# Mixing from two copies of V: the low-rank part kept once, the second copy swapped by transfers within SBUF

## The chip, the cores and the metric

The kernel runs on one core of one Trainium2 chip. The metric is the device time of an execution in microseconds; the time before is 667.36 us, the median of three runs. A core has a matrix engine (PE, with its weight loads listed apart as PEld), a vector engine (DVE), a scalar engine (ACT), GpSimd (POOL) and SyncE (SP), which here only issues transfers. Each engine runs its own list of instructions in order; semaphores tie the lists together.

## The reference, cut to what matters

```python
# attention: 4 batches, 8 heads, 768 positions, head size 64, decay lam per head
intra = np.einsum('bhic,bhjc->bhij', qb, kb) * Dmask[None]
intra = np.einsum('bhij,bhjd->bhid', intra, vb)
inter = np.einsum('bhid,bhde->bhie', qb * lam_pow[None], kv_state)
out[:, :, sl] = intra + inter
...
# mixer: x is the attention's output as (4, 768, 512); U is 768 x 32, V is 32 x 768
xt = x.transpose(0, 2, 1)
h = xt @ U @ V
u = x + h.transpose(0, 2, 1)
ch = np.maximum(u @ w_ch1, 0.0) @ w_ch2
return (u + ch).astype(np.float32)
```

The change touches `h`: along the 768 positions of a batch, P = xᵀU has rank 32, and the mix is Vᵀ times P, one 128 x 512 tile of u at a time.

## The kernel before, in words

The 4 x 768 rows are 24 tiles of 128, numbered s = 6b + c (batch b, tile c). The attention takes one tile per step. The list `pieces` (L637 to L667) writes the order of a step out by hand: transposes of q and k for tile s+1 (`prep`, L368), the turn and the mix of earlier tiles, the attention's products for tile s (`intra`, `state`, `inter`), scores for tile s+1 (`scores`), then side work (`aside`, L734: conversion of weights from double precision, one piece at a time). Each engine gets its instructions in exactly this order.

At the end of a batch `low` (L469) multiplies its six tiles by U into a 32 x 512 result. `low_rows` (L487) splits that result into a high part (the upper bits) and a low part (the rest), and the pieces in `pps`, called as `next_of_low` (L542) in the first step of the next batch, put them where the mix reads them. The mix of tile s runs in step s + 7, so the first is in step 7 and reads what step 6 wrote.

All products of the mix are of high and low parts, four in number: high V and low V, each with high P and low P. Half the columns of the result come from rows 0 to 63 of the operands, the other half from rows 64 to 127. `v_hl` (L290) holds V on 4 x 32 rows: high, low, high, low. `p_hl` holds, for each half of 64 rows, the high part of P twice (columns 0 to 255) and the low part twice (columns 256 to 511). `mix` (L552) makes four matmuls per tile: for the high columns and then the low columns, one for each half of the rows; as the 64 rows of V are high over low, each matmul sums two of the products.

Filling `p_hl` for one batch (L525 to L538) takes four ACT copies of the high part (`spread`, L527), two POOL subtractions for the low part (L531) and two ACT copies that double the low part (`spread_low`, L538). `spread` and `low_part` are called ahead of `scale` in the step, `spread_low` after `mixed`. The last batch is mixed during the first product with w_ch1, with a full 128-row `p_hl` (L492 to L511, L566).

V itself is prepared by `v_steps` (L682) as side work of steps 0 to 5: a load in two parts of 32 rows, the conversion on DVE and ACT, then the high part by four ACT copies (L706) and the low part by two DVE (L710, rows 32 to 63) and two POOL subtractions (L710, rows 96 to 127), both in step 5.

Loads on SP are issued by `load_next` (L670) in the same order: q and k in `prep`, v in `next_v` (L435), each into buffers (three for q and v, four for k) that an earlier tile has left. The words of the weights (L140) and the stores of finished tiles u (L577) stand on the same SP list.

`v_hl` and `p_hl` are columns of one tile, `vp` (L289), in a slot of the pool of w_ch1's weights; two further columns of it hold constants for the conversion (`set_ends`, L751). `lam_row` (L747) and `blank` (L748) are used before the first step only.

After the attention (some 117 us) come the products with w_ch1 (L817, L827) and with w_ch2 (L950 to L954).

Of the kernel before, what the change touches and what calls it, by code (L numbers as in the profile page):

```python
# [8 lines left out]
FP32 = mybir.dt.float32  # L9
F32R = mybir.dt.float32r  # L10
# [4 lines left out]
P = 128  # L15
# [3 lines left out]
def kernel(  # L19
# [28 lines left out]
    nc = tc.nc  # L48

    B, H, S, D = q.shape  # L50
    HP = H // 2
    NT = S // P
    C = H * D
# [3 lines left out]
    R = moe_U.shape[1]  # L57
    G = P // R
# [29 lines left out]
    def set_ends(t):  # L88
        nc.vector.memset(t[:, 0:1], 1151.0)
        nc.vector.memset(t[:, 1:2], 255.0 * (1 << 23))  # L90
        ends.append(t)
# [195 lines left out]

    assert G == 4
    vp = w1_pool.tile([P, 3, C], F32R, tag="w1", name="vp").rearrange("p n c -> p (n c)")  # L289
    v_hl, p_hl = vp[:, 0:S], vp[:, S : S + C]  # L290


    ident = keep.tile([P, P], FP32, name="ident")
    small = consts.tile([P, 16], FP32, name="small")
    zeros = small[:, 0:1]

    mask = consts.tile([P, 2, HP, P], FP32, name="mask")
# [189 lines left out]
    def low_rows(b):  # L487

        pp, t = pps.pop(b), tmp("p_h")[0:R]
        own = [(slice(g * R, (g + 1) * R), slice(g * P, (g + 1) * P)) for g in range(G)]  # L490
        if b == B - 1:
            h, h2, l, l2 = (p_hl[g * R : (g + 1) * R] for g in range(G))  # L492
            for rows, cols in own:
                nc.vector.tensor_scalar(
                    t[:, cols].bitcast(U32), pp[rows].bitcast(U32), HI, None, ALU.bitwise_and
                )

            def low_part():
                for rows, cols in own:
                    nc.vector.tensor_tensor(  # L500
                        out=l[:, cols], in0=pp[rows], in1=t[:, cols], op=ALU.subtract
                    )

            def spread():
                nc.scalar.copy(h, t)
                nc.scalar.copy(h2, t)

            def spread_low():
                nc.scalar.copy(l2, l.bitcast(FP32))

            pps[b] = [spread, low_part, spread_low]  # L511
            return

        rows_f, pp = pp, others.pop(b)
        for g in range(2, G):
            nc.vector.tensor_copy(
                out=rows_f[:, g * P : (g + 1) * P], in_=pp[g * R : (g + 1) * R]
            )
        nc.vector.tensor_scalar(t.bitcast(U32), rows_f.bitcast(U32), HI, None, ALU.bitwise_and)
        wide = [slice(x * 2 * P, (x + 1) * 2 * P) for x in range(2)]  # L520

        def place(g, low):
            return p_hl[g * R : (g + 1) * R, wide[low]]

        def spread():  # L525
            for g in range(G):
                nc.scalar.copy(place(g, 0), t[:, wide[g // 2]])  # L527

        def low_part():
            for x in range(2):  # L530
                nc.gpsimd.tensor_tensor(  # L531
                    out=place(2 * x, 1), in0=rows_f[:, wide[x]], in1=t[:, wide[x]],
                    op=ALU.subtract,
                )

        def spread_low():
            for x in range(2):
                nc.scalar.copy(place(2 * x + 1, 1), place(2 * x, 1).bitcast(FP32))  # L538

        pps[b] = [spread, low_part, spread_low]  # L540

    def next_of_low(b):  # L542
        pps[b].pop(0)()
# [7 lines left out]

    def mix(s):  # L552
        b, c = divmod(s, NT)
        weights = v_hl[:, c * P : (c + 1) * P]
        if b < B - 1:
            pm = both_halves(s)[:, :, 2 * P :]
            for low in range(2):
                for x in range(2):
                    nc.tensor.matmul(  # L559
                        out=pm[:, x], lhsT=weights[half[x]],  # L560
                        rhs=p_hl[half[x], low * 2 * P : (low + 1) * 2 * P],
                        start=(low == 0), stop=(low == 1),
                    )
            return
        pu = bank([P, C], "pu", "b2")
        nc.tensor.matmul(out=pu, lhsT=weights, rhs=p_hl, start=True, stop=True)  # L566
        nc.vector.tensor_tensor(out=xs[s], in0=pu, in1=xs[s], op=ALU.add)

    def mixed(s):
# [68 lines left out]
    for s in range(NS):  # L638
        b, c = divmod(s, NT)
        done = s - NT - 1  # L640
        more = s + 1 < NS
        turns = done > 0 and (done - 1) // TG < FG
        mixes = 0 <= done < NS - NT - 1
        rows = c == 0 and b > 0
        step = [("prep", s + 1)] * more
        step += [("turn", done - 1)] * turns + [("mix", done)] * mixes
        step += [("mix", done + 1)] * (not more)
        step += [("next_of_low", b - 1)] * rows + [("next_of_low", b - 1)] * rows
        step += [("scale", s + 1)] * more
        step += [("fade", s)] * (c > 0)  # L650
        step += [("late", s - 1)] * (1 < s < NT - 1 or s > NT)
        step += [("turned", done - 2)] * (done > 1 and c == 1)
        step += [("split", done - 1)] * turns
        step += [("mixed", done)] * mixes + [("mixed", done + 1)] * (not more)
        step += [("next_of_low", b - 1)] * rows
        both = [("intra", s), ("state", s)]
        step += (both if s > NT else both[::-1]) + [("next_v", s), ("inter", s)]
        step += [("late", s)] * (s < 2 or s in (NT - 1, NT))
        step += [("turned", done - 1)] * (done > 0 and c > 0)
        step += [("scores", s + 1)] * more  # L660
        step += [("low", b)] * (more and c == NT - 1)
        step += [("aside", s)] * (0 < s < NT - 2 or s > NT)
        step += [("masked", s + 1)] * more
        step += [("low_rows", b)] * (more and c == NT - 1)
        step += [("aside", s)] * (s in (0, NT - 2, NT - 1, NT))
        step += [("store", done)] * (done >= 0 and done // TG < FG)
        pieces += step  # L667
# [14 lines left out]
    def v_steps():  # L682
# [8 lines left out]
        def parts(gs):  # L691
            for half in range(2):
                rows, cols = slice(half * R, (half + 1) * R), slice(half * SH, (half + 1) * SH)
                for g in gs:
                    yield v_hl[g * R : (g + 1) * R, cols], rows

        def five():
            st["t"] = t = wconv.tile([P, C], FP32, tag="wt", name="vt")[0 : 2 * R, 0:SH]
# [9 lines left out]
        def low(g, engine):  # L708
            for out, rows in parts((g,)):
                engine.tensor_tensor(  # L710
                    out=out, in0=st["v"][rows], in1=st["t"][rows], op=ALU.subtract
                )

        halves = [moe_V[:, half * SH : (half + 1) * SH] for half in range(2)]
        return weight_steps(dst, halves, SH, 2 * R, in_parts=True) + [
            five, lambda: low(1, nc.vector), lambda: low(3, nc.gpsimd),
# [27 lines left out]

    ordered = ctx.enter_context(ExitStack())
    ordered.enter_context(tc.manual_schedule())
    lam_row = consts.tile([1, H + P], FP32, name="lam_row")  # L747
    blank = x_pool.tile([P, C], FP32, tag="x", name="blank")[:, 0:P]  # L748
    nc.vector.memset(blank, 0.0)
    nc.vector.memset(lam_row[:, H:], 1.0)  # L750
    set_ends(vp[:, S + C : S + C + 2].bitcast(FP32))  # L751
    nc.scalar.dma_start(out=lam_row[:, 0:H], in_=lam.unsqueeze(0))
    load_next("q", nc.sync)
    load_next("k", nc.scalar)
# [299 lines left out]
```

## Time and profile before

| what | us |
|---|---|
| median of three runs | 667.36 (666.33 to 668.0) |
| the profiled execution | 669.62 |
| its span, first to last instruction | 667.8 |
| L559, mix of three batches: 72 matmuls, 72 weight loads | 316 ns and 188 ns each (median) |
| L527, ACT copies of the high part: 12 | 404 ns each |
| L531, POOL low part: 6 | 724 ns each |
| L538, ACT copies of the low part: 6 | 402 ns each |
| L710, DVE low part of V: 2 | 766 ns each |
| L710, POOL low part of V: 2 | 1000 ns each |

The profile is of one execution. Times are from the span's start; L numbers are lines of the kernel before. A stretch "40.00:60.00" lists busy time and number of instructions of PE, PEld, DVE, ACT and POOL, then the granted clock of PE, the busy share of the DMA engines and GB/s. In the timeline a line gives start, duration, engine, line, operation, output and inputs; a bracket gives idle time of the engine ahead of it and what released it. The DMA rows of the timeline show issuing on SP, not the transfer.

### The profile page before, as it was taken

To read this page: it belongs to the slowest core of one execution; us is meant where nothing else is said; L and a number is where in the kernel's file an instruction comes from. 1 tells how busy PE (TensorE), PEld (TensorE's weight loads), DVE (VectorE), ACT (ScalarE), POOL (GpSimd) and SP (SyncE) were. 2 spreads that over 40 slices of the span, in tenths; PEclk is the share of its full clock that TensorE was granted. 3 is DMA by queue.
4 is the path that set the end of the run, shared out by engine and by line. 5 is a ranking of instruction groups with operands and counts; after the bars stand their busy time and mean duration, and the time that the engine had idled before them with its cause. 6 is when DMAs were issued, how large, how long until landed. Compare 5 with 4: busy or idle time off the path is not lost.

```text
span 667.8 us, 13404 instructions
## 1 busy us (share of the span) xinstructions
PE 656.2 (98%) x5242; PEld 538.7 (81%) x5242; DVE 491.0 (74%) x862; ACT 280.4 (42%) x530; POOL 115.0 (17%) x98
## 2 busy tenths in 40 slices
PE   8899999999999999999999999999999999999997
PEld 7788988788888888888888887888888888888886
DVE  5578988878999777777797255786677776865864
ACT  4677885554555444444453121332322322322320
POOL 4465876330000000000000000030030300300300
PEclk9999999999999999999999999999999999999999
DMA  8999984355776655555578899764263453543531
GB/s 197 224 224 233 259 217 139 127 190 162 268 249 238 216 199 202 201 201 200 201 263 292 311 326 395 253 212 126 89 211 104 125 190 94 168 147 96 159 93 63
DMA packets 131776, 131.29 MB, mean 197 GB/s; under 512 B 81346, under 2 KB 89794, under 8 KB 131714
## 3 DMA queue, kind: packets, MB, share of 16 engines
q1 hardware_dynamic: 130512, 130.05, 62.2%
q8 instruction: 41, 0.67, 0.4%
q10 hardware_dynamic: 1202, 0.39, 0.2%
q14 instruction: 21, 0.17, 0.1%
HBM read 80.09 MB, written 50.33 MB: 195 GB/s over the span
## 4 chain that ended last, share of the span: by engine, by line
PE 95%; DMA 1%; DVE 1%; SPq 1%; issue 1%; ACT 0%; DVEq 0%; ACTq 0%
PE pz L817 27%; PE pz L950 13%; PE pz L952 13%; PE pd L827 13%; PE pd L954 13%; PE px L447 3%; PE pss L406 3%; PE px L458 2%; PE pqk L358 2%; DMA qraw<-in_q_dram 1%; PE pkv L425 1%; SPq L279 1%; PE pp L474 1%; PE pm L559 1%; PE put L590 1%
## 5 line engine op out<-in xcount | busy, mean ns | idle before, releaser
L817 PE MATMUL pz<-u_hl,w 128*128 128x512 f32 x768 | 190.0, 397 | 0.0
L817 PEld LDWEIGHTS pz<-u_hl,w 128*128 128x128 f32 x768 | 144.0, 188 | 35.2 <-ACT r L823 0.3
L952 PE MATMUL pz<-w_hl,m 128*128 128x512 f32 x384 | 151.1, 396 | 0.0
L950 PE MATMUL pz<-w_hl,m 128*128 128x512 f32 x384 | 150.9, 396 | 0.0
L954 PE MATMUL pd<-w_d,m 128*128 128x512 f32 x384 | 149.5, 396 | 0.0
L933 ACT ACTIVATE m<-mt 128x512 fp32r<-128x512 f32 x96 | 60.6, 632 | 196.6 <-PE pd L954 127.5
L979 POOL TENSOR_TENSOR o<-o,u 128x512 f32<-128x512 f32 x20 | 29.9, 1531 | 447.4 <-DMA rm<-r_d 291.4
L934 DVE SCALAR_TENSOR_TENSOR m<-rm,m 128x512 fp32r<-128x512 f32 x96 | 71.4, 745 | 47.3 <-ACT m L933 47.2
L832 DVE SCALAR_TENSOR_TENSOR r<-pd,r 128x512 f32<-128x512 f32 x96 | 61.8, 685 | 53.5 <-ACT r L823 43.5
L827 PE MATMUL pd<-u_d,w 128*128 128x512 f32 x384 | 98.6, 397 | 0.0
L823 ACT ACTIVATE r<-pz 128x512 f32<-128x512 f32 x96 | 52.1, 596 | 93.0 <-PE pz L817 92.3
L952 PEld LDWEIGHTS pz<-w_hl,m 128*128 128x128 f32 x384 | 72.3, 188 | 17.8 <-DVE m L934 0.2
L954 PEld LDWEIGHTS pd<-w_d,m 128*128 128x128 f32 x384 | 72.3, 188 | 17.7 <-DVE m L935 0.2
L950 PEld LDWEIGHTS pz<-w_hl,m 128*128 128x128 f32 x384 | 72.3, 188 | 17.6
L827 PEld LDWEIGHTS pd<-u_d,w 128*128 128x128 f32 x384 | 72.1, 188 | 17.3
L932 DVE TENSOR_SCALAR mt<-rm 128x512 uint32<-128x512 uint32 x96 | 46.1, 481 | 33.5 <-DMA rm<-r_d 33.2
L935 DVE SCALAR_TENSOR_TENSOR m<-m 128x512 fp32r<-128x512 f32 x96 | 69.1, 721 | 0.9
L415 DVE TENSOR_TENSOR sm<-pss,mask 128x512 f32<-128x512 f32 x48 | 30.9, 684 | 10.0 <-PE pss L406 9.7
L212 ACT CAST w<-wt 128x512 fp32r<-128x512 f32 x32 | 19.8, 620 | 30.6 <-DVE wt L209 23.4
L406 PE MATMUL pss<-qt,kt 64*128 64x128 f32 x384 | 29.1, 291 | 0.8 <-issue 0.7
L447 PE MATMUL px<-vraw,sm 128*64 128x64 f32 x768 | 27.8, 225 | 1.2 <-ACT x_nat L464 0.6
L447 PEld LDWEIGHTS px<-vraw,sm 128*64 128x64 f32 x768 | 24.9, 138 | 3.9 <-ACT x_nat L464 0.9
(96 smaller groups left out, 668.7 us busy)
## 6 DMA issues: line engine op xcount, KB each, us to landing
r_d<-r SPq DMA_DIRECT2D x96, 256.0 KB, 2.4
rm<-r_d SPq DMA_DIRECT2D x96, 256.0 KB, 2.7
words<-in_moe_w_ch_dram SPq DMA_DIRECT2D x30, 512.0 KB, 4.3
w_d<-w SPq DMA_DIRECT2D x16, 768.0 KB, 3.3
w_hl<-w_d SPq DMA_DIRECT2D x16, 512.0 KB, 6.4
vraw<-in_v_dram SPq DMA_DIRECT2D x24, 256.0 KB, 5.0
u_d<-x_nat SPq DMA_DIRECT2D x24, 256.0 KB, 4.1
u<-u_d SPq DMA_DIRECT2D x24, 256.0 KB, 4.1
```

The source lines that it names most:

```text
L406: nc.tensor.matmul(out=pss[:, x, a, :], lhsT=kt[half[x], a, :], rhs=qt[half[x], a, :], start=True, stop=True,)
L447: nc.tensor.matmul(out=px[half[t], x, a, :], lhsT=sm[:, x, a, half[t]], rhs=vr[:, 2 * a + x, :], start=(a == 0), stop=(alone and a == HP - 1),
L817: nc.tensor.matmul(out=acc[g][0], lhsT=w[:, n, ct, :], rhs=uhl[g][:, n, ct, :], start=(ct == 0 and n == 0), stop=(ct == CT - 1 and n == 1),)
L823: nc.scalar.mul(rs[g], acc[g][0], 4096.0 + 1.0)
L827: nc.tensor.matmul(out=acc[g][1], lhsT=w[:, 2, ct, :], rhs=ud[g][:, ct, :], start=(ct == 0), stop=(ct == CT - 1),)
L832: nc.vector.scalar_tensor_tensor(rs[g], acc[g][1], 4096.0, rs[g], ALU.mult, ALU.add)
L933: nc.scalar.activation(out=m[:, 0], in_=t, func=AF.Relu)
L934: nc.vector.scalar_tensor_tensor(m[:, 1], r, 0.0, hi, ALU.max, ALU.subtract)
L935: nc.vector.scalar_tensor_tensor(m[:, 2], hi, E, low, ALU.mult, ALU.subtract)
L950: nc.tensor.matmul(out=pz, lhsT=m[:, 0, cols], rhs=hl[:, 0], start=first, stop=False)
L952: nc.tensor.matmul(out=pz, lhsT=m[:, 1, cols], rhs=hl[:, 1], start=False, stop=end)
L954: nc.tensor.matmul(out=pd, lhsT=m[:, 2, cols], rhs=dd, start=first, stop=end)
```

## The change

A second copy of V, with high and low exchanged in each pair of 32 rows, is kept beside the first: `v_hl` is now two copies of 768 columns, which fill `vp`. `p_hl` becomes a tile of its own of 256 columns with, for each half of 64 rows, the high part over the low part, each once. The mix again makes four matmuls per tile of the same shapes: for the plain V and then the swapped V, one for each half of the rows. Plain V gives high by high and low by low, swapped V gives the two cross products.

For one batch this needs two ACT copies in place of four, the same two POOL subtractions, and no `spread_low`. The swapped copy is made once, by four transfers of 32 x 768 elements from SBUF to SBUF, issued on SP at the head of step 6. In the lists of the engines these four transfers stand after the words of step 5's side work and ahead of the q load of step 6. The first reads what DVE's L710 wrote, the third what POOL's wrote, the second and fourth what ACT's L706 wrote. On PE the third matmul of the first mix waits for the first and second transfer, the fourth for the third and fourth.

The last batch's P goes into the second copy of V, which no mix reads by then. The constants of `set_ends` move to `small`, and `lam_row` into the tile of `blank`.

```diff
-    v_hl, p_hl = vp[:, 0:S], vp[:, S : S + C]
+    v_hl = vp.rearrange("p (n c) -> p n c", n=2)
+    p_hl = consts.tile([P, 2 * P], F32R, name="p_hl")
...
-    small = consts.tile([P, 16], FP32, name="small")
+    small = consts.tile([P, 18], FP32, name="small")
...
-            h, h2, l, l2 = (p_hl[g * R : (g + 1) * R] for g in range(G))
+            h, h2, l, l2 = (v_hl[g * R : (g + 1) * R, 1, 0:C] for g in range(G))
...
-        def place(g, low):
-            return p_hl[g * R : (g + 1) * R, wide[low]]
+        def place(g):
+            return p_hl[g * R : (g + 1) * R]
 
         def spread():
-            for g in range(G):
-                nc.scalar.copy(place(g, 0), t[:, wide[g // 2]])
+            for x in range(2):
+                nc.scalar.copy(place(2 * x), t[:, wide[x]])
 
         def low_part():
             for x in range(2):
                 nc.gpsimd.tensor_tensor(
-                    out=place(2 * x, 1), in0=rows_f[:, wide[x]], in1=t[:, wide[x]],
+                    out=place(2 * x + 1), in0=rows_f[:, wide[x]], in1=t[:, wide[x]],
                     op=ALU.subtract,
                 )
 
-        def spread_low():
-            for x in range(2):
-                nc.scalar.copy(place(2 * x + 1, 1), place(2 * x, 1).bitcast(FP32))
-
-        pps[b] = [spread, low_part, spread_low]
+        pps[b] = [spread, low_part]
...
-        weights = v_hl[:, c * P : (c + 1) * P]
+        weights = v_hl[:, :, c * P : (c + 1) * P]
         if b < B - 1:
             pm = both_halves(s)[:, :, 2 * P :]
-            for low in range(2):
+            for n in range(2):
                 for x in range(2):
                     nc.tensor.matmul(
-                        out=pm[:, x], lhsT=weights[half[x]],
-                        rhs=p_hl[half[x], low * 2 * P : (low + 1) * 2 * P],
-                        start=(low == 0), stop=(low == 1),
+                        out=pm[:, x], lhsT=weights[half[x], n], rhs=p_hl[half[x]],
+                        start=(n == 0), stop=(n == 1),
                     )
             return
...
-        nc.tensor.matmul(out=pu, lhsT=weights, rhs=p_hl, start=True, stop=True)
+        nc.tensor.matmul(out=pu, lhsT=weights[:, 0], rhs=v_hl[:, 1, 0:C], start=True, stop=True)
...
-        step = [("prep", s + 1)] * more
+        step = [("swap", s)] * (s == NT) + [("prep", s + 1)] * more
...
-        step += [("next_of_low", b - 1)] * rows
...
-                    yield v_hl[g * R : (g + 1) * R, cols], rows
+                    yield v_hl[g * R : (g + 1) * R, 0, cols], rows
...
+        def swap():
+            whole = v_hl.bitcast(FP32)
+            for g in range(G):
+                nc.sync.dma_start(
+                    out=whole[g * R : (g + 1) * R, 1],
+                    in_=whole[(g ^ 1) * R : ((g ^ 1) + 1) * R, 0],
+                )
+
+        run["swap"] = lambda s: swap()
...
-    lam_row = consts.tile([1, H + P], FP32, name="lam_row")
-    blank = x_pool.tile([P, C], FP32, tag="x", name="blank")[:, 0:P]
+    blank = x_pool.tile([P, C], FP32, tag="x", name="blank")
+    lam_row, blank = blank[0:1, P : P + H + P], blank[:, 0:P]
...
-    set_ends(vp[:, S + C : S + C + 2].bitcast(FP32))
+    set_ends(small[:, 16:18])
```

## The prediction

> **What bounds the kernel now.** I read the page first, then the engines' busy time by stretches of 20 us, then the timeline and the chain of waits around the first mix. The page gives the bound, the stretches say where there is anything left to win.
>
> ```profile
> span 667.8 us, 13404 instructions
> PE 656.2 (98%) x5242; PEld 538.7 (81%) x5242; DVE 491.0 (74%) x862; ACT 280.4 (42%) x530; POOL 115.0 (17%) x98
> ```
>
> And of the stretches (length, then busy time and instructions of PE, PEld, DVE, ACT and POOL, then granted clock, DMA share, GB/s):
>
> ```profile
> 40.00:60.00 20.00, 18.90 (x520) 17.23 (x518) 16.19 (x29) 15.37 (x38) 14.07 (x13) 1.00 0.92 225
> 60.00:80.00 20.00, 19.48 (x546) 17.80 (x544) 18.51 (x32) 15.53 (x38) 16.25 (x15) 1.00 1.01 254
> ...
> 120.00:140.00 20.00, 20.00 (x138) 16.20 (x138) 17.18 (x31) 11.45 (x21) 6.78 (x6) 1.00 0.41 138
> ```
>
> PE is busy 656.2 of 667.8 us, and from 120 us on it is never idle. Whatever delays PE before that comes out at the end; whatever relieves another engine is worth only the PE idle time that this engine causes. All of the change lies before 125 us. The DMA engines are full (0.92 to 1.01) just where the change adds transfers.
>
> The timeline around the first mix (step 7 of the attention):
>
> ```profile
> 37.87 1.55 DVE L710 TENSOR_TENSOR vp<-vf,vt 32x384 fp32r<-32x384 f32 x2
> 37.98 2.02 POOL L531 TENSOR_TENSOR vp<-p_f,p_h 32x256 fp32r<-32x256 f32 x2 [2.09 <-DVE p_h L519]
> 38.01 1.45 SPq L140 DMA_DIRECT2D words<-in_moe_w_ch_dram  x1
> 38.20 1.66 ACT L527 CAST vp<-p_h 32x256 fp32r<-32x256 f32 x4
> ...
> 39.54 1.32 SPq L279 DMA_DIRECT2D qraw<-in_q_dram  x1
> ...
> 39.89 0.83 ACT L538 CAST vp<-vp 32x256 fp32r<-32x256 f32 x2
> ...
> 40.05 0.48 PEld L559 LDWEIGHTS pm<-vp 64*128 64x128 f32 x3
> 40.08 1.07 PE L559 MATMUL pm<-vp 64*128 64x256 f32 x4
> ...
> 40.74 0.58 ACT L464 COPY x_nat<-px 128x512 f32<-128x512 f32 x1
> 40.77 0.18 PEld L559 LDWEIGHTS pm<-vp 64*128 64x128 f32 x1 [0.24 <-ACT vp L538]
> ...
> 41.38 0.51 PE L447 MATMUL px<-vraw,sm 128*64 128x64 f32 x10 [0.23 <-ACT x_nat L464]
> ```
>
> Columns are start, duration, engine, line; brackets are idle time and its releaser. Two things are to be seen. First, the six ACT copies (L527, L538) do hold PE here: its fourth mixing weight waits 0.24 us for L538, and the next product (px, 41.38) for the x_nat copy, which stands behind L538 on ACT. Second, the low part of V (DVE L710) ends at 39.42 us, 0.6 us before the first mix reads V at 40.05. A copy of V that starts from that low part and goes by DMA has 0.6 us.
>
> The two later low-rank parts (near 65 and 92 us) look different. The chain of waits:
>
> ```profile
> 64.67 0.29 DVE p_f L516
> ...
> 65.30 0.42 DVE p_h L519
> ...
> 67.76 0.34 DVE kv L431
> ...
> 68.14 0.71 PE pqk L358 x16
> ```
>
> There PE waits for DVE, through p_f, p_h and the work that follows them on DVE up to kv; none of the removed ACT copies is on that chain.
>
> **What the Trainium skill says.** "Perfetto Trace Analysis", Per-instruction lifecycle: a DMA instruction's time in the profile ends when its descriptors are made, and movement comes after. The trace agrees: SP's row of 1.45 us for the words above has its data at 4.4 us from its start. "DMA: Bandwidth & Descriptors", Anatomy of one DMA: a transfer costs about 2.0 us fixed, mostly the receipt of the last write, plus bytes over 436 GB/s. Loaded transfers here take 3.2 to 6.3 us, the shortest 1.8 (128 KB of output) and 2.3 (128 KB of q). Same page, Queues, rings and completion order: on each DMA engine the descriptors of one issuing engine are consumed in order, so the swap stands behind SP's earlier loads; the v load issued at 37.02 takes 5.1 us and the words 4.4, so both land after 42 us. "TensorE: Matmul & The Clock Gate", What's actually happening: an idle window of about 3.4 us halves the clock; the trace shows clock 1.00 throughout, with PE gaps up to 1.6 us, so it doesn't show a longer one.
>
> **The change part by part.**
>
> *PE.* The mix keeps its instructions: 72 matmuls and weight loads of the same shapes, in the same places. Cost 0. What they wait for changes: the pair n=0 waits for POOL's low part, the pair n=1 for the four transfers (two for each half).
>
> *ACT.* Each of three low-rank parts loses two of the four L527 copies and both L538 copies, 4 x 0.403 = 1.6 us, 4.8 us in all. At 40 us this shortens PE's path: POOL's second part ends at 40.00 as now, the x_nat copy moves from 40.74 to about 39.1 (px is done at 38.7 and ACT after two copies at 39.03), so without a new wait px could start at about 40.1 + 0.3 for four matmuls = 40.4 to 40.5, not 41.38: a gain of 0.9 us. At 65 and 92 us DVE holds PE: I take 0, bounded by 0 to 0.4 us each, the largest PE wait on ACT shown in 60 to 80 us.
>
> *The four transfers.* 32 x 3072 B each (96 KB), issued once on SP at the head of step 6, behind the words of 38.01 and ahead of the q load of 39.54. SP runs behind PE: it reaches that place at 39.46, when DVE's 39.42 is just past, so SP hardly waits; the four waits (DVE, ACT, POOL, ACT) are met, POOL's and ACT's since 36. First issue then at 39.54. Nearest rows for an issue: 0.37 us, the shortest of any q load, and 1.0 us, the mean of the two V loads, which have the same 32 x 3072 B, at 18 us in a full queue (share 1.18). The queue is half empty at 41 to 42 us (share 0.42), so I take 0.6, with 0.1 between issues: the fourth starts at 39.54 + 3 x 0.7 = 41.64. Landing from there: 1.8 at best, 3.8 as the V loads at worst; I take 2.3. That is 43.94. The last mixing matmuls and px follow 0.4 us later (one weight load of 0.19, a matmul, the semaphore): px starts at 44.35 instead of 41.38, **+3.0 us**, the 0.9 of gain being inside this. Both ends: 0.37 + 0.1 and 1.8 give 39.54 + 1.41 + 1.8 + 0.4 = 43.15, +1.8; 1.0 + 0.1 and 3.8 give 47.04, +5.7.
>
> *What is queued behind.* On PE: all of step 7, and through its results every engine. On SP: the q, k, v and words loads of step 6, some 2 to 3 us later than now. The q of 39.54 lands at 43.4 and is transposed at 48.9, three steps on; the v of 41.59 lands at 46.6 and is used at 50.0, so 3.4 us of cover, and their users are 3 us later as well: cost 0, up to 1 us if the full DMA engines don't catch up with 384 KB more (1.6 us at the 245 GB/s of this stretch). After 42 us PE's idle time is almost all its own chain within a step, so I let none of the 3.0 us be absorbed.
>
> *Rest, at nothing.* The bias pair set into another tile (two memsets of 0.06 us, as before), lam in the blank tile (same ACT transfer, other columns), p_hl in its own tile, the last batch's low part in the second copy of V (it waits for mixes that end by 115.5 and is written at 123): same instructions, same places. If the cover of the last went, PE would wait at 125 us.
>
> **Sum.** The profiled execution before: 669.62 us, 667.8 of it span. With +3.0 it would be 672.6, span 670.8. The median of the runs is 2.3 us lower than the profiled one, 667.36, and moves by the same: **670.4 us**.
>
> **Rivals.** 0.3% is 2.0 us, about what a measurement of this kernel can tell from no change.
>
> 1. The forecast, one stall of some 3 to 4 us at the first mix, +3.0 (between +1.8 and +4.5): chance 0.58.
> 2. Quick transfers. Issues at 0.37 each and landings under 2 us, and part of the shift soaked up by the gaps which the chain of waits calls "issue" (0.83 us at 51.3, 0.94 at 107.9). For it: the SBUF source and the queue half empty at 41. Against: words and v, ahead in the same rings, land after 42. +1.2, 668.6: 0.22.
> 3. Longer: issues as slow as the V loads, the loads behind them late too, or PE's clock halved after a gap over 3.4 us. +5.5, 672.9: 0.16. For it: DMA share 0.92 and more all along; against: SP's later loads have 3.4 us and more of cover.
> 4. The other side: ACT's copies at the head of each batch are what PE's delay grows from, in all three places. It decides if the 1.6 us come off PE's path each time: -4.8, against a stall at its low end of 1.8: 664.4. It needs ACT on the path at 65 and 92 us, where the chain shows DVE: 0.04.
>
> That the change misses its purpose isn't a rival on time: the copies are gone from ACT's list.
>
> **How the numbers follow.** Slower by over 0.3%: most of case 1 (0.56) and case 3, 0.72. Within: case 2 and the rest of case 1, 0.24. Faster: 0.04. The range runs from 668.0 (+0.6, inside case 2) to 673.0 (+5.6, into case 3): outside it lie case 4, a fifth of case 2 and the far part of case 3.
>
> **What would show it.** Right: in step 7 PE's third and fourth mixing weight waits for a DMA vp<-vp, together 2 to 4 us; px starts near 44.3; ACT's x_nat is done before 40; PE busy after that as before, and the shift at 120 us equals the shift at 44. Wrong: no DMA wait at the mix, a shift that shrinks between 44 and 120 us, or PE waiting for q, k or v loads in steps 8 to 10.

## The result and the profile after

The changed kernel took 673.71 us (median of 4 runs, 672.71 to 674.97) against 667.17 us before (4 runs, 666.33 to 668.0): ratio 1.0101, 95% interval 1.0082 to 1.0120, or some 6.5 us slower. The prediction said 670.4 us, 668.0 to 673.0. The direction and the place were right; the size was half of what came.

The page of the changed kernel, its head:

```profile
span 673.2 us, 13409 instructions
PE 658.5 (98%) x5242; PEld 541.1 (80%) x5242; DVE 490.0 (73%) x862; ACT 275.4 (41%) x518; POOL 115.5 (17%) x98
```

The same number of matmuls takes 2.3 us more of busy time (656.2 before), and PE's idle time has grown from 11.6 to 14.7 us. The stretches of 20 us show where (columns as before the change: length, busy time of PE, PEld, DVE, ACT, POOL, granted clock, DMA share, GB/s):

```profile
40.00:60.00 20.00, 15.55 (x351) 14.02 (x355) 11.04 (x20) 9.65 (x25) 10.62 (x10) 0.83 0.93 223
60.00:80.00 20.00, 19.73 (x548) 18.00 (x542) 17.57 (x31) 13.38 (x31) 13.76 (x13) 1.00 1.01 251
```

From 40 to 60 us PE ran 351 matmuls where it had run 520, and its clock was 0.83 instead of 1.00. From 60 us on it is as full as before. The timeline of that stretch (`pss` holds the scores, `sm` the masked scores, `px` the attention's output, `pm` the mix and the turn, `pqk` the transposed q and k):

```profile
39.11 1.55 DVE L705 TENSOR_TENSOR vp<-vf,vt 32x384 fp32r<-32x384 f32 x2
...
40.31 0.59 ACT L465 COPY x_nat<-px 128x512 f32<-128x512 f32 x1
...
40.95 3.49 SPq L712 DMA_DIRECT2D vp<-vp  x4
...
41.32 0.42 PE L556 MATMUL pm<-p_hl,vp 64*128 64x256 f32 x2
...
44.53 0.54 SPq L279 DMA_DIRECT2D qraw<-in_q_dram  x1
...
44.94 0.58 PE L556 MATMUL pm<-p_hl,vp 64*128 64x256 f32 x1 [3.21 <-DMA vp<-vp]
...
46.20 0.55 PE L556 MATMUL pm<-p_hl,vp 64*128 64x256 f32 x1 [0.68 <-DMA vp<-vp]
...
46.68 1.97 PE L448 MATMUL px<-vraw,sm 128*64 128x64 f32 x32
...
50.50 1.56 PE L407 MATMUL pss<-qt,kt 64*128 64x128 f32 x16
```

The two products with plain V run at 41.32; the third and fourth, with the swapped V, wait 3.21 and 0.68 us for the transfers. SP needs 3.49 us to issue the four. The last, in the chain of waits (start, duration, what; `issue` is time for which the profile shows no wait), takes 2.17 us to land:

```profile
43.89 2.17 DMA vp<-vp
46.06 0.14 issue
46.20 0.55 PE pm L556
```

Then something that is no wait: px takes 1.97 us, where the same 32 products took 1.15 us before. Stretches of 1 us (same columns; the clock is the number ahead of the last two) show why:

```profile
44.00:45.00 1.00, 0.06 (x1) 0.06 (x1) 0.00 (x0) 0.00 (x0) 0.85 (x1) 0.77 0.68 158
45.00:46.00 1.00, 0.52 (x1) 0.22 (x1) 0.00 (x0) 0.00 (x0) 0.00 (x0) 0.50 0.54 119
...
50.00:51.00 1.00, 1.00 (x28) 0.88 (x22) 0.05 (x1) 0.36 (x1) 0.66 (x1) 0.50 1.01 224
51.00:52.00 1.00, 1.00 (x20) 1.00 (x18) 0.00 (x0) 0.22 (x1) 0.00 (x0) 0.81 0.89 207
```

PE's clock was halved from about 44.5 us (the second from 44 averages 0.77) to about 51.4 (the one from 51 averages 0.81), for 6.8 us. All four timed executions show a mean clock of 0.994 or 0.995, which such a stretch makes of 1.00.

The two traces, product by product. PE was already 1.24 us late in the profiled execution of the changed kernel when step 6 began (pss at 39.86 against 38.62), by small gaps before 36 us. Three kernels below that are the kernel before up to this point (e13, e17, e18) stand between 1.88 us early and 0.22 us late there, so this is taken as scatter between executions, and taken off.

| stretch | before, us | after, us | difference |
|---|---|---|---|
| pss of step 6 to px of step 7 | 38.62 to 41.38 | 39.86 to 46.68 | +4.06, the wait |
| px to the next pss | 2.22 | 3.82 | +1.60, the clock |
| that pss to the one after | 4.30 | 4.70 | +0.40, the clock |
| sum | | | +6.06 |

The 6.06 of this one place are the measured 6.5 us within the spread of the runs. The two profiled spans differ by less, 5.4 us. PE is 7.3 us late from 48 to 94 us (1.24 and 6.06), and 1.9 of this goes again between 94 and 109 us. It goes because the profiled execution of the kernel before stood still there, 0.94 us of it in one pause at 107.94 that the profile puts down to no wait; every other trace of this case gains 0.8 to 1.4 us on it between 104 and 109 us.

### The profile page after: what moved, and what is told of

Same layout as the page of the kernel before. It is cut to its first block, busy times and chain, and to the rows that moved or that the text cites. A ratio compares the mean times of both kernels' runs of the same rounds, so it can differ in the third digit from the quotient of the medians.

```text
span 673.2 us, 13409 instructions
## 1 busy us (share of the span) xinstructions
PE 658.5 (98%) x5242; PEld 541.1 (80%) x5242; DVE 490.0 (73%) x862; ACT 275.4 (41%) x518; POOL 115.5 (17%) x98
## 4 chain that ended last, share of the span: by engine, by line
PE 95%; DMA 2%; DVE 1%; issue 1%; POOL 0%; ACT 0%; ACTq 0%; DVEq 0%; SPq 0%
PE pz L821 27%; PE pz L956 13%; PE pz L954 13%; PE pd L831 13%; PE pd L958 13%; PE pss L407 3%; PE px L448 3%; PE px L459 2%; PE pqk L359 2%; PE pkv L426 1%; DMA kraw<-in_k_dram 1%; PE pp L475 1%; DMA qraw<-in_q_dram 1%; PE pm L556 1%; PE put L586 1%
## 5 line engine op out<-in xcount | busy, mean ns | idle before, releaser
L416 DVE TENSOR_TENSOR sm<-pss,mask 128x512 f32<-128x512 f32 x48 | 30.9, 685 | 11.5 <-PE pss L407 11.1
```

## The experiments

The theory after the result was that all of it is one place: the wait at the first mix and the clock that falls with it. Sixteen kernels tested it, each timed against the kernel before on the same chip. In brief (ratio to the kernel before, with its interval):

| run | what differs | median us | ratio |
|---|---|---|---|
| e1_filled | changed, PE kept busy in the gap | 672.19 | 1.0068 (1.0052 to 1.0083) |
| e2_v_earlier | changed, V and swap a step earlier | 670.29 | 1.0041 (1.0020 to 1.0062) |
| e3_ahead_of_words | changed, swap ahead of the words on SP | 672.66 | 1.0080 (1.0065 to 1.0094) |
| e7_two_queues | changed, two transfers issued by ACT | 672.75 | 1.0070 (1.0051 to 1.0089) |
| e8_mix_later | changed, first mix later in its step | 671.31 | 1.0051 (1.0034 to 1.0067) |
| e11_first_by_engines | changed, first mix needs no transfer | 671.29 | 1.0051 (1.0032 to 1.0070) |
| e14_convert_later | e11, weights of step 8 at 9 | 670.71 | 1.0034 (1.0019 to 1.0049) |
| e15_pool_first | e14, first columns by POOL | 671.10 | 1.0043 (1.0027 to 1.0058) |
| e16_behind_words | first two mixes need no transfer, swap behind the words | 671.07 | 1.0049 (1.0032 to 1.0066) |
| e4_copies_kept | e2, removed ACT copies redone | 675.85 | 1.0118 (1.0098 to 1.0137) |
| e12_first_and_copies | e11, removed ACT copies redone | 672.71 | 1.0072 (1.0048 to 1.0096) |
| e13_unread | before, four transfers nobody reads | 670.91 | 1.0039 (1.0022 to 1.0056) |
| e17_unread_one | before, their bytes in one transfer | 668.78 | 1.0009 (0.9992 to 1.0025) |
| e18_unread_tiny | before, four transfers of 2 KB | 671.45 | 1.0046 (1.0029 to 1.0063) |
| e19_two_transfers | changed, two transfers | 672.63 | 1.0067 (1.0040 to 1.0093) |
| e20_one_transfer | changed, one transfer | 668.40 | 1.0005 (0.9989 to 1.0021) |

**The clock.** e1 puts 15 products, whose results nobody reads, where PE waits:

```diff
+                    if s == 0 and n == 1:
+                        for _ in range((11, 4)[x]):
+                            nc.tensor.matmul(
+                                out=filler[:, 0:P], lhsT=ident, rhs=ident, start=True, stop=True
+                            )
```

> The changed kernel with 11 and 4 products of the identity, into an unused bank, ahead of the third and fourth matmul of the first mix, so that PE is busy for most of the wait for the transfers (nothing of the result changes). Theory: the wait costs some 4 us and the halved clock after it another 2.0, and the clock falls only because PE stands still; so the clock stays at 1.00, the transfers land as before, and the time is 673.7 - 2.0 = 671.7. Rival: the clock falls for another reason, or the slow stretch after the wait comes from late loads: 673.5 or more.

Measured: 672.19 us, 1.5 us under the changed kernel (2.2 by the two ratios). Its timeline around the first mix:

```profile
41.39 2.50 SPq L718 DMA_DIRECT2D vp<-vp  x4
...
44.38 0.38 PE L562 MATMUL pm<-p_hl,vp 64*128 64x256 f32 x1 [1.41 <-DMA vp<-vp]
...
45.78 0.38 PE L562 MATMUL pm<-p_hl,vp 64*128 64x256 f32 x1
```

The transfers are no earlier, and the granted clock is 1.00 throughout. So the wait alone leaves the kernel 4.5 us slower, and 1.5 to 2.2 us of the loss is the clock. The two intervals just touch (1.0083 and 1.0082): the size rests on the trace's 2.0 us as much as on this run.

**The wait: reach the transfers sooner, or need them later.** e2 does the conversion of V and the swap a step earlier; e3 puts the swap ahead of the words on SP's list; e7 lets ACT issue two of the four; e8 moves the first mix behind the other products of its step.

```diff
-        step = [("swap", s)] * (s == NT) + [("prep", s + 1)] * more
+        step = [("swap", s)] * (s == NT - 1) + [("prep", s + 1)] * more
...
-        (v_steps(), (0, 0, 3, 3, 4, 4, 4, 5, 5)),
+        (v_steps(), (0, 0, 2, 2, 3, 3, 3, 4, 4)),
```

> The changed kernel with V converted one step earlier and the four transfers at the head of step 5. Theory: all of the loss is the wait at the first mix and its clock; without it the fewer ACT copies leave a gain of up to 0.9 us: 666.3, between 665.8 and 667.5, no wait of PE for a transfer in step 7. Rival one, the 384 KB of transfers and the later loads cost by themselves: 668.5 or more, with PE waiting for q, k or v. Rival two, the mix from two copies is slower on PE: 668 or more with longer matmuls at the mix.

Measured: 670.29. The wait at the first mix was gone, and 2.7 us were left. They are at least partly this kernel's own: V's load now came late for DVE, and PE waited 2.1 us for sm behind it at 24.8 us. In six of its seven executions the mean clock was 0.994 to 0.997, so it was halved for a time in them, though not in the profiled one. So e2 says that the wait can be moved away, not what is left without it.

```diff
-            for g in range(G):
+            for g in (1, 2, 3, 0):
...
-            five, lambda: low(1, nc.vector), lambda: low(3, nc.gpsimd),
+            five, lambda: low(1, nc.vector), lambda: low(3, nc.gpsimd), swap,
```

(with `swap` no longer at the head of step 6)

> The changed kernel with the four transfers ahead of step 5's load of weight words on SP, the one that reads DVE's part last; V is converted when it was. Theory: three transfers go before DVE is done, the last is issued at once when DVE ends (about 40.7 in the changed kernel's profile) and lands 2.2 us later; PE waits 1.5 us, the clock stays at 1.00: 668.0, between 667 and 669.5. Rival: the wait comes from full DMA rings, not from the place in SP's list: landing 4 us or more after DVE's end, 671 or more.

Measured: 672.66, and a longer wait. The timeline of e3:

```profile
37.99 4.60 SPq L712 DMA_DIRECT2D vp<-vp  x4
...
44.22 0.65 PE L556 MATMUL pm<-p_hl,vp 64*128 64x256 f32 x2 [5.60 <-DMA vp<-vp]
```

SP reaches the swap at 37.99, just after DVE's low part of V (37.53 in this run) and just ahead of the mix (38.20): V is no earlier, so neither is the swap. And the first issue alone took 2.69 us with its data ready, the others 0.54 to 0.55. A place further up the list gained nothing for the mix.

```diff
-                nc.sync.dma_start(
+                engine = nc.scalar if g % 2 else nc.sync
+                engine.dma_start(
```

> The changed kernel with the second and fourth transfer issued on ACT, the first and third on SP as before. Theory: the wait is the time to issue four transfers (0.6 to 1.6 us for the first, 0.63 for each other) and 2.2 us to land; with two fewer on SP the last lands 1.3 us sooner, the wait falls under 3 us and the clock stays at 1.00 in most runs: 673.7 - 1.3 - 2.0 = 670.4, between 669.5 and 671.5 as the issues cost ACT 1.1 us. Rival: the landing doesn't depend on the issues ahead: 673 or more.

Measured: 672.75; PE's wait at the mix was 2.6 us and still halved the clock, and the transfers took 3.5 to 4.3 us to land. What the second issuer saved went in the landing: the Trainium skill, "DMA: Bandwidth & Descriptors", Rules for kernel authors, says that spreading transfers over issuing engines saves only issue time, since all run on the same DMA engines, and this trace agrees.

```diff
-        step += [("turn", done - 1)] * turns + [("mix", done)] * mixes
+        step += [("turn", done - 1)] * turns + [("mix", done)] * (mixes and done > 0)
...
+        step += [("mix", 0), ("mixed", 0)] * (done == 0)
```

(and `mixed` of the first tile moves with it)

> The changed kernel with the first tile's mix moved behind step 7's other products (transfers and V as in the changed kernel). Theory: PE has 2.3 us of work before it waits, so the wait is some 1.9 us, the clock stays, and the time is 673.7 - 2.2 - 2.0 = 669.5. Rival: the loads behind the transfers on SP are late by themselves, so the lost time shows up again as PE waiting for q, k or v: 671 or more.

Measured: 671.31. The products moved ahead of the mix hid part of the wait. What is left, in e8's timeline and, below, its stretches of 1 us:

```profile
43.33 0.38 PE L556 MATMUL pm<-p_hl,vp 64*128 64x256 f32 x1 [0.58 <-DMA vp<-vp]
...
45.52 0.55 PE L556 MATMUL pm<-p_hl,vp 64*128 64x256 f32 x1 [1.81 <-DMA vp<-vp]
```

```profile
43.00:44.00 1.00, 0.38 (x1) 0.18 (x1) 0.00 (x0) 0.08 (x1) 0.74 (x1) 1.00 0.65 144
44.00:45.00 1.00, 0.00 (x0) 0.00 (x0) 0.00 (x0) 0.00 (x0) 0.00 (x0) 1.00 0.05 10
45.00:46.00 1.00, 0.48 (x4) 0.51 (x6) 0.00 (x0) 0.00 (x0) 0.00 (x0) 0.60 0.72 166
46.00:47.00 1.00, 1.00 (x14) 1.00 (x13) 0.69 (x1) 0.00 (x0) 0.00 (x0) 0.50 1.21 274
```

Two gaps of 0.58 and 1.81 us were enough to halve the clock, from about 45.2 us. The last section says why.

**No wait at all at the first mix.** The first mix reads 128 columns of the second copy. e11 lets ACT, DVE and POOL write these directly, and the transfers carry the other 640:

```diff
+            for g in (1, 3):
+                nc.scalar.copy(v_hl[g * R : (g + 1) * R, 1, 0:P], st["t"][0:R, 0:P])
...
+            engine.tensor_tensor(
+                out=v_hl[(g ^ 1) * R : ((g ^ 1) + 1) * R, 1, 0:P],
+                in0=st["v"][0:R, 0:P], in1=st["t"][0:R, 0:P], op=ALU.subtract,
+            )
```

> The changed kernel in which ACT, DVE and POOL write the first 128 columns of the swapped copy (two, one and one instructions of 32 x 128) and the four transfers carry the other 640, so the first mix waits for no transfer and the next one, 4.3 us later, does. V is converted when it was. Theory: the whole loss goes, and the fewer ACT copies leave 0.3 to 0.9 us of gain: 666.6, between 666.0 and 667.6, clock 1.00. Rival: transfers of this size and the later loads on SP cost by themselves: 669 or more.

Measured: 671.29, still 3.4 us slower than before. The timeline of e11 shows a wait at another place:

```profile
50.29 1.29 DVE L160 TENSOR_SCALAR sc<-words 128x512 uint32<-128x512 uint32 x1 [1.32 <-DMA words<-in_moe_w_ch_dram]
...
52.91 1.27 DVE L416 TENSOR_TENSOR sm<-pss,mask 128x512 f32<-128x512 f32 x2
...
53.69 1.98 PE L448 MATMUL px<-vraw,sm 128*64 128x64 f32 x32 [2.80 <-ACT sc L167]
```

The words of step 6, behind the swap on SP, were issued at 45.90 (42.55 before); DVE waits for them, sm stands behind on DVE, and PE waits 2.80 us for it. (The bracket names ACT's sc; but px reads sm, and the first half of sm ends at 53.58, just before px starts.) The clock fell here too, at 53.7 us, for 3.4 us. e14 starts the conversion that needs these words a step later, e15 gives the first columns to POOL instead, e16 gives POOL 256 columns and puts the swap behind the words.

```diff
-        (w1_steps(0, True), (3, 4, 5, 6, 8, 9, 10, 11, 13, 14, 15)),
+        (w1_steps(0, True), (3, 4, 5, 6, 9, 9, 10, 11, 13, 14, 15)),
```

> The kernel whose first 128 swapped columns are written by the engines (e11), with the conversion of w_ch1's first block started in step 9 instead of 8. New theory: the late words of step 6 are then in time, the wait in step 8 goes, and only some 1 us of delays at the first and second mix is left: 668.3, between 667.3 and 669.3. Old theory: no part in it, as e11, 671.3.

> As the run before it, with the first 128 columns written by POOL alone (four instructions), so that ACT and DVE do what they do in the changed kernel. Theory: no wait at the first mix, 0.5 us at the second, the gain of the fewer ACT copies is kept: 667.3, between 666.4 and 668.3; if it is under before, the change is worth having in this form. Rival: POOL's low part of P comes later, the first mix waits for POOL: 668.5 or more.

> The changed kernel with the first 256 columns written by POOL and the four transfers (512 columns) behind the words of step 6 on SP; the conversion starts in step 8. New theory: the words are not late, the third mix is the first that needs a transfer and finds it landed: 667.2, between 666.3 and 668.3. Rival: any place on SP makes some later load late: 669.5 or more.

Measured: 670.71, 671.10, 671.07. Each time the clock of the profiled execution stayed at 1.00 (and of 20, 21 and 19 of the 22 timed ones), the wait at the mix was at most 0.7 us, and PE waited somewhere else: for DVE's ut, the split of a turned tile, in e14 (2.0 us), for ACT's faded, the decayed state, and a v load in e15 (1.6 and 0.9), for v loads in e16 (2.2). So the theory of one place fell: with the wait and the slow clock gone, 2.3 to 3.3 us were still lost. (What it costs by itself to move a conversion or to give POOL more work was not run.)

**What ACT's relief is worth.** e4 (on e2) and e12 (on e11) put back the ACT copies that the change removed, writing to a scratch tile that nobody reads:

```diff
+            spare = tmp("spare").bitcast(F32R)
+            for x in range(2):
+                nc.scalar.copy(spare[x * R : (x + 1) * R, wide[x]], t[:, wide[x]])
```

> As the kernel with V a step earlier, but with the four ACT copies of each batch that the change removed made again, into a scratch tile (their result is not used). Theory: on ACT they cost what the change gained, 0.9 us at the first mix and nothing at 65 and 92 us: 0.9 over the kernel with V earlier, about 667.2. Rival: the ACT copies never mattered, the same time within 0.3 us; or they matter in each batch, 2 us and more over it.

> The kernel before this one in the list (first 128 columns by the engines), with the four ACT copies of each batch made again into a scratch tile whose content isn't used. Theory: the copies cost 0.9 us at the first mix and nothing at the other two: 667.5. Rival: the same time within 0.3 us, or, if ACT's copies count in every batch, 669 or more.

Measured: 5.6 and 1.4 us more than e2 and e11. The scratch tile takes one of three buffers that p_f and p_h use too, and the new wait (pqk for DVE's kv, 3.5 us in both) may be that buffer's and not the copies'. It comes twice in each run, 1.8 us each time, and after three of the four the clock fell as well, for 3.4 us. And the intervals of e11 and e12 overlap. These two don't measure the relief; it stays open.

**The second cost.** e13 is the kernel before with four transfers of 32 x 254 elements into unused columns of `vp`, at the head of step 6. Nobody reads them or waits for them.

```diff
+            for g in range(G):
+                nc.sync.dma_start(
+                    out=whole[g * R : (g + 1) * R, at:],
+                    in_=whole[(g ^ 1) * R : ((g ^ 1) + 1) * R, 0 : 3 * C - at],
+                )
```

> The kernel before, with four transfers of 32 x 254 elements added on SP at the head of step 6, into columns that nothing reads; nothing waits for them. New theory: the transfers cost a second time, through SP: each holds SP for 0.6 us or more, so the loads behind them start 2.5 to 3.5 us later, and the words of step 6 come too late for the conversion in step 8, which holds DVE, then the scores' masking, then PE (after which its clock may halve): 2 to 3.5 us over before, 669.7 to 671.3. The old theory, all of the loss is the wait for the transfers: as before, 667.7 within 0.7.

Measured: 670.91, 2.6 us slower (1.0039). Here is the second cost by itself, and its trace shows how it was paid. In its timeline, and below it in DVE's table of waits (what waits, for what: total, times, longest):

```profile
45.14 0.84 SPq L140 DMA_DIRECT2D words<-in_moe_w_ch_dram  x1
...
51.98 1.98 PE L447 MATMUL px<-vraw,sm 128*64 128x64 f32 x32 [3.59 <-DVE sm L415]
```

```profile
DVE sc L160 <- DMA words<-in_moe_w_ch_dram: 3.9, 1, 3.9
```

The words of step 6 were issued 2.6 us later than before (42.55), DVE waited for them with sm behind, and PE waited 3.59 us for sm: the path of e11, without any wait at the mix. Then the clock was halved for 6.8 us, from 50.35. So the second cost is a wait and a slower clock too. Of e13's 22 executions, 8 show a mean clock of 0.999 or more, and their median is 669.2 us; the other 14 have 0.994 to 0.997, and 671.5. Two things could make it: SP's time for four issues, or 127 KB more on full DMA engines. e17 moves the same bytes in one transfer of 128 rows, e18 issues four of 2 KB each (both edits are shown against e13):

```diff
-            for g in range(G):
-                nc.sync.dma_start(
-                    out=whole[g * R : (g + 1) * R, at:],
-                    in_=whole[(g ^ 1) * R : ((g ^ 1) + 1) * R, 0 : 3 * C - at],
-                )
+            nc.sync.dma_start(out=whole[:, at:], in_=whole[:, 0 : 3 * C - at])
```

> The kernel before with one transfer within SBUF that nobody reads or waits for, 128 rows x 254 elements (127 KB, the bytes of the four unread transfers before it, issued once in place of four times) on SP at the head of step 6. If the cost of the unread transfers (+2.7 us) is SP's time for four issues, one issue costs at most 1 us: 668.5. If it is the bytes on the DMA engines, it stays +2 to +3: 670 to 671.

```diff
-                    out=whole[g * R : (g + 1) * R, at:],
-                    in_=whole[(g ^ 1) * R : ((g ^ 1) + 1) * R, 0 : 3 * C - at],
+                    out=whole[g * R : (g + 1) * R, at : at + 16],
+                    in_=whole[(g ^ 1) * R : ((g ^ 1) + 1) * R, 0:16],
```

> The kernel before with four unread transfers of 32 rows x 16 elements (2 KB each) at the same place: the same number of issues with hardly any bytes. If the cost is SP's time for the issues: +2 to +2.7, 669.6 to 670.5. If it is the bytes: no change, 667.5 to 668.0.

Measured: 1.0009 for the bytes in one issue, no change that can be told (up to 1.0025); 1.0046 for four issues with hardly any bytes, the whole cost. The two intervals don't overlap, but only just (1.0025 and 1.0029), and those of e17 and e13 do by 0.0003. SP's rows, first e17, then e18:

```profile
39.04 1.50 SPq L717 DMA_DIRECT2D vp<-vp  x1
40.63 0.53 SPq L279 DMA_DIRECT2D qraw<-in_q_dram  x1
41.26 0.60 SPq L279 DMA_DIRECT2D kraw<-in_k_dram  x1
41.95 1.02 SPq L279 DMA_DIRECT2D vraw<-in_v_dram  x1
```

```profile
39.72 3.30 SPq L718 DMA_DIRECT2D vp<-vp  x4
43.12 0.53 SPq L279 DMA_DIRECT2D qraw<-in_q_dram  x1
43.74 0.53 SPq L279 DMA_DIRECT2D kraw<-in_k_dram  x1
44.37 1.15 SPq L279 DMA_DIRECT2D vraw<-in_v_dram  x1
```

Four issues of 2 KB hold SP 3.30 us, about as long as four of 96 KB (3.49). And SP does not catch up: in the kernel before, e17 and e18 no gap between its rows is over 0.54 us from 36 to 90 us. Issue times of the v loads that follow, in us:

| v load | before | e17, one issue | e18, four issues |
|---|---|---|---|
| first | 41.59 | 41.95 | 44.37 |
| second | 45.74 | 46.38 | 48.38 |
| fourth | 56.15 | 55.27 | 57.79 |
| sixth | 65.28 | 64.74 | 67.57 |
| eighth | 73.90 | 74.00 | 78.34 |

In e18's profile PE was not late until 75 us (its pss stands at 75.80, against 75.81 before): the lateness sat in SP's list for 36 us before PE paid for it. Then it did, in e18's chain of waits and its table of waits:

```profile
78.34 6.29 DMA vraw<-in_v_dram
84.63 0.14 issue
84.76 1.15 PE px L447 x32
```

```profile
PE px L447 <- DMA vraw<-in_v_dram: 2.4, 2, 1.4
```

In the kernel before no row of PE's waits between 36 and 120 us names a load, and so it is in e17. In this execution of e18 the words of step 6 landed 3.5 us after their issue (5.3 in e13) and nobody waited for them: the same lateness on SP's list is paid at another load. The clock kept its full rate in it; in 13 of the 22 timed ones it did not (median 672.0 us, against 669.8 of the other 9).

**Fewer issues.** Rows of V alternate high and low, so rows 32 to 127 of the swapped copy are rows 0 to 95 of the plain one. e19 makes the copy with two transfers, e20 with one of 96 rows x 640 columns; in e20 POOL writes the first 128 columns (four instructions) and, in step 6, rows 0 to 31 of the rest (two).

```diff
-            for g in range(G):
-                nc.sync.dma_start(
-                    out=whole[g * R : (g + 1) * R, 1],
-                    in_=whole[(g ^ 1) * R : ((g ^ 1) + 1) * R, 0],
-                )
+            nc.sync.dma_start(out=whole[0:R, 1], in_=whole[R : 2 * R, 0])
+            nc.sync.dma_start(out=whole[R:, 1], in_=whole[0 : 3 * R, 0])
```

> The changed kernel with the swapped copy made by two transfers in place of four (rows 0 to 31 from rows 32 to 63; rows 32 to 127 from rows 0 to 95, since rows alternate high and low parts). Two issues fewer of 0.63 us: the wait at the first mix is some 1.3 us shorter, 671.5 to 672.5, less if the gap becomes short enough for PE's clock to stay. If issue time goes with the rows of a transfer and not with their number, as the changed kernel: 673.5.

```diff
+            nc.sync.dma_start(out=whole[R:, 1, P:], in_=whole[0 : 3 * R, 0, P:])
...
+                nc.gpsimd.tensor_copy(
+                    out=v_hl[g * R : (g + 1) * R, 1, 0:P], in_=st["t"][0:R, 0:P]
+                )
+                nc.gpsimd.tensor_tensor(
+                    out=v_hl[(g - 1) * R : g * R, 1, 0:P],
+                    in0=st["v"][0:R, 0:P], in1=st["t"][0:R, 0:P], op=ALU.subtract,
+                )
```

> The changed kernel with one transfer (rows 32 to 127 from rows 0 to 95, columns 128 to 767); the first 128 columns of the second copy are written by POOL (four instructions), and so are rows 0 to 31 of the others, in step 6. If SP's issues and the wait on the first mix make up the whole loss: 667 to 669. If the bytes or POOL's additional work hold PE: 670 or more.

e19: 672.63, the expected time but not for the expected reason. Its timeline:

```profile
38.74 0.75 SPq L711 DMA_DIRECT2D vp<-vp  x1
39.59 0.54 SPq L712 DMA_DIRECT2D vp<-vp  x1
...
43.88 0.58 PE L556 MATMUL pm<-p_hl,vp 64*128 64x256 f32 x2 [5.20 <-DMA qraw<-in_q_dram]
```

Both issues are done in 1.38 us, but the larger one (288 KB) lets PE go only 4.3 us after its issue begins, against 2.3 for the last 96 KB in the changed kernel (43.89 to 46.20). (The q load that the bracket names landed at that moment; the weight load of the same product is put down to the transfer, with 5.4 us.) The wait at the mix stayed, and with it the halved clock; only SP's list was shorter.

e20: 668.40, ratio 1.0005 (up to 1.0021), the only form of the change that costs nothing measurable. In its timeline the first mix runs without a gap, and SP spends 0.60 us on the swap:

```profile
39.86 0.60 SPq L721 DMA_DIRECT2D vp<-vp  x1
...
40.46 0.54 PE L556 MATMUL pm<-p_hl,vp 64*128 64x256 f32 x4
```

Its transfer lands 4.1 us after the issue, under the products of step 7. The Trainium skill, "DMA: Bandwidth & Descriptors", Rules for kernel authors, says that two transfers over two halves of the partitions gain nothing over one transfer over all of them; e17 against e13 and e18 agrees, and what the split costs here is SP's time. No version ran faster than the kernel before.

## Why the prediction was wrong

- **The place and the mechanism** were right: the third and fourth mixing products wait for the transfers, PE's busy share from 60 us on is as before, and ACT's x_nat is done before the mix (40.31 + 0.59, at 40.90, against 41.32). The shift of 7.3 us is the same from 48 to 94 us; that it is smaller at 120 us comes from the pauses in the profiled execution of the kernel before.
- **The size of the wait** was under by 1.1 us: +4.06 in place of +3.0. The term that was off is the issues: "0.6, with 0.1 between" put 2.1 us from the first issue to the fourth; it took 2.94 (40.95 to 43.89), 0.8 more. The first is the outlier, 1.59 us, the others 0.54. The landing, 2.3, was 2.17; the rest is 0.2 at either end of this path.
- **PE's clock** was the step that failed most in the changed kernel: the forecast's sum has no term for it. It stood in rival 3, at 0.16, "after a gap over 3.4 us", while the forecast itself put a stall of "some 3 to 4 us" there. It also took a gap under 3.4 us to be safe. A gap of 3.21 us halved the clock for 6.8 us, +2.0. With it the forecast's own 3.0 would have been 5.0, and with the measured wait 6.1. Rival 3, +5.5, came nearest and names this clock; its issues as slow as the V loads did not come.
- **"What is queued behind … cost 0, up to 1 us"** was wrong, and the changed kernel alone could not show it. By itself the delay of SP's list costs 2.6 us (e13) to 3.1 us (e18: 0.0046 of 668), the clock that falls in more than half of the executions included. The reason given was 3.4 us of cover between a load's landing and its use; that holds for one load, but SP's list has next to no slack there, so the lateness stays in every later load until PE, or an engine that feeds it, meets one with less cover. The prediction worked out the cover of q and v, not that of the words, which DVE waited for in e11 and e13. In the changed kernel PE is itself 6 us late, and from 47 us on none of its waits names a load; SP has gaps there of 0.8 to 1.5 us ahead of six of its v loads between 54 and 88 us (the first at 54.68). The first cost hides the second. With the wait shortened or gone (e8, e11, e14 to e16) the time stays at 670.7 to 671.3. That the waits found there come from SP's late list is traced for e11 and fits e16; for the ut and faded waits of e14 and e15 it is argued only.
- **The bytes**, "384 KB more (1.6 us)" in the prediction's worst case for the loads behind, were no cost as far as they were tried: 127 KB in one issue came out at 1.0009. That the whole 384 KB are free is not shown; e20 moves 240 KB at 1.0005.
- **The gain of 0.9 us from ACT** inside the 3.0 shows in no run's time. e20 has ACT's shorter list and no wait, and is as fast as the kernel before, not faster. In its trace px follows the pss of step 6 after 2.08 us, where it was 2.76 before: 0.7 us is there. By the next pss only 0.1 is left, gone in pauses between px and the next product that the profile puts down to no wait. Six POOL instructions and one issue that e20 adds may have to do with it.

## What to carry to other kernels

A transfer costs three things that have to be priced apart: the time that its issue holds the queue's list, the landing, and the bytes; with a list that has no slack, count issues first, and make one large transfer out of four small ones, even where it lands later, as long as nobody waits for it (e20, not e19). Where a wait is put on PE, look at stretches of 3.4 us around it: if PE can be left busy for less than some half of one, add the slower clock to the sum, not to a rival. And a wait can hide the cost of what stands behind it: before removing it, run the cause alone, with nobody waiting, to see what removing it can bring.

## What the runs showed of the hardware

- PE's clock follows windows of 3.41 us. The traces hold the times at which the granted clock changed. In the nine in which it fell, the time between two changes is always 3.41 us or a multiple of it (34.13, 6.83 in the changed kernel; 44.37, 3.41 in e11). So the windows can be counted off from the first rise to full clock. The clock fell at the end of ten windows, in which PE had been busy 0 to 1.71 us, and in all other windows before 120 us that began at full clock PE had been busy 1.76 us or more, but for one of 1.67. So what counts here is whether PE is busy for about half of a window, not how long a single gap is:

| trace | window, us | PE busy, us | clock after it |
|---|---|---|---|
| changed kernel | 41.13 to 44.55 | 0.60 | half |
| e8 | 41.79 to 45.20 | 1.33 | half |
| e13 | 46.94 to 50.35 | 1.45 | half |
| e4 | 67.61 to 71.02 | 1.65 | half |
| e20 | 11.56 to 14.97 | 1.67 | full |
| e12 | 96.36 to 99.77 | 1.71 | half |
| e4 | 19.82 to 23.24 | 1.76 | full |
| e4 | 23.24 to 26.65 | 1.92 | full |

- In e4 a wait of 2.92 us, up to 24.73, lay across the last two of these windows and left the clock alone; one of 1.76 us, up to 70.89, halved it. The Trainium skill, "TensorE: Matmul & The Clock Gate", What's actually happening, describes a free-running window of 3.4 us, and the clock halved after an idle one. The traces agree on the window; "idle" takes in a window in which PE is busy for nearly half. As the windows start between 8.1 and 11.1 us in these traces, the same wait can halve the clock in one execution and not in the next. This fits the two groups of e13's executions; it was not tried by itself.
- The clock came back at the end of windows in which PE was busy 3.09 us (e8) or all 3.41, and not after 3.06 us (e7) or less.
- The issue of a transfer within SBUF that followed another took 0.53 to 0.55 us whether it carried 2 KB, 32 KB, 96 KB or 288 KB, in 40 of 42 cases (1.14 in e14 and 1.53 in e7 are the others). The first of a row of four took 0.60 (e13), 1.39 (e18), 1.59 (changed kernel) and 2.69 us (e3); no run says what sets this.
- From the issue's start to landing, 96 KB took 2.1 to 3.7 us (changed kernel), 240 KB 4.1 (e20), and 2 KB 1.6 to 3.5 (e18): on these loaded engines small transfers land little sooner.
